# Windowed attention and a mixture of experts: the tiles that join two batches become plain 256-column tiles, in another order

## The chip, the cores and the metric

The kernel runs on one core of one Trainium2 chip. Its engines are TensorE (PE; its weight loads are listed apart as PEld), VectorE (DVE), ScalarE (ACT), GpSimd (POOL) and SyncE (SP, which issues most DMAs). The metric is the device time of one execution in microseconds (us), lower is better.

## The reference

In short: causal attention with a window of 128 keys and a bias by distance, and then a mixture of experts in which each token goes to one expert.

```python
batch, n_heads, seq, head_dim = (4, 8, 576, 64)
...
scores = scale * np.matmul(q, k.transpose(0, 1, 3, 2))
rel = pos[:, None] - pos[None, :]
bias = slopes[:, None, None] * (-np.abs(rel).astype(np.float32))[None, :, :]
mask = (rel >= 0) & (rel < window)
scores = np.where(mask, scores + bias[None], -1000000000.0)
attn = softmax(scores)
x = np.matmul(attn, v)
...
N, D, E, F = (2304, 512, 8, 1024)
expert_idx = np.argmax(x @ w_gate, axis=1)
h = np.maximum(np.einsum('ecd,edf->ecf', disp, w1), 0.0)
y = np.einsum('ecf,efd->ecd', h, w2)
out[i] = gate_w[i] * y[expert_idx[i], pos[i]]
```

## The kernel before

**Tiles.** 576 rows of a batch are four tiles of 128 rows and a rest of 64. The rests of two batches share one tile of 128 rows, the joined tile (`i == 4` in `TILES`), so there are 18 tiles: for each pair of batches nine, the fifth of them joined (numbers 4 and 13). A query row sees at most 128 keys back, so tile i needs the keys of chunks i-1 and i: 256 columns, and 128 in the four first tiles of a batch.

**Steps of a tile.** `turn_raw` turns raw k and q by products with the identity; `turn_hi` (ACT) and `turn_lo` (DVE) split the turned block into two f16 parts. `qk` makes scores of four heads into two PSUM banks, with three f16 products for each head (high-high, low-high, high-low); the two heads of a 128-row chunk lie in rows 0 to 63 and 64 to 127 of PE and come in pairs in the trace (x2). `softmax` (DVE) adds the table `tab` of bias and mask and finds the largest score, `expo` (ACT) makes `p`. For two heads at a time, `ptrans` turns `p` on PE into `pt`, `pevac` copies it into `pT`, and `pv` multiplies by v (65 columns: v and a column that sums). `xden`, `xrec`, `xnorm` divide, `xput` writes the rows to `xd` in DRAM, `xtrans`, `xevac`, `logits` make the gate's logits. An f32 product of `pv`, `logits` is two passes in the trace.

**The joined tile before.** `qM` and `pM` are 256 wide with zeros, so that queries of batch z stand in their 64 columns of block z and zeros elsewhere. `qk` runs each product for both batches on 192 keys (128 of chunk 3 and the last 64) into the same columns. `pv` then has four products for each head, two of them with 64 rows:

```python
ops = [(z, *x) for z in range(2 if i == 4 else 1) for x in key_chunks(ti)]
for y, (z, ci, vi, n) in enumerate(ops):
    PE.matmul(
        xv[:, h % 4, 0:D + 1], lhsT=s["pT"][:n, ci, a, 128 * z:128 * z + 128], rhs=vS[:n, (b0 + z) % 2, vi, h, 0:D + 1],
```

**Routing and experts.** When the rows of a batch of tiles have logits, `route_ops` ranks them (`o_rank` on PE), and POOL, PE and DVE make lists of tokens by expert. After the third of five batches (tiles 9 to 12 and half of 13) the first two experts begin: `gather` of their rows, `x_hi`, `x_lo`, two DMA transposes (`x_tr`), and `up` (PE, line 743). The weights of these two are split into f16 parts (`w_hi` on ACT, `w_lo` on DVE, line 677 and 681) during attention.

**Order.** Everything up to the first two experts is planned by `Plan`: each step has an engine, a time and a key; a list scheduler with a model of the clock, of transfers and of queues runs in the program's build and puts the steps of each engine in the order in which it would start them. Keys are shifted by the table `KEYS`. On the chip each engine takes its steps in that order, whatever time they need. The other six experts follow in written order.

**Lines on PE.** `turn_raw` 287, `qk` 331, `ptrans` 361, `pv` 387, `xtrans` 421, `logits` 443, `o_rank` 498, `o_list` 571, `up` 743; in the changed kernel 293, 339, 369, 393, 424, 446, 501, 574 and 746. `softmax` is line 346, `x_hi` 710, `x_tr` 719.

Of the kernel before, what the change touches and what calls it, by code (L numbers as in the profile page):

```python
# [43 lines left out]
C_N = C_T + 448  # L44
# [136 lines left out]
def attention_moe(ctx, tc, q, k, v, w_gate, w1, w2, capacity, const, out):  # L181
# [24 lines left out]
    tab = cp.tile([128, H, 448], BF16, name="tab")  # L206
# [16 lines left out]
    vS = kt.tile([128, 2, 5, H, DV], F32, name="vS")  # L223
# [18 lines left out]
    def setup_v():  # L242
        POOL.memset(vS[:, :, :, :, D:DV], 1.0 / XS)
# [930 lines left out]
```

## Time and profile before

| | us |
|---|---|
| median of 3 runs (lowest to highest) | 486.26 (482.13 to 494.63) |
| the profiled execution, its own time | 487.78 |
| its span (first to last instruction) | 486.0 |
| PE busy, DVE busy, ACT busy | 448.7, 245.0, 236.3 |
| attention, until the first expert's first product | 241.4 |

The profiled execution lies 1.5 us above the median of the runs, and 1.8 us of its time lie outside its span. [...] A busy PE in the profile includes pipelined instructions that overlap, so it shows where PE idles rather than how fast it works.

### The profile page before, as it was taken

To read this page: it belongs to the slowest core of one execution; us is meant where nothing else is said; L and a number is where in the kernel's file an instruction comes from. 1 tells how busy PE (TensorE), PEld (TensorE's weight loads), DVE (VectorE), ACT (ScalarE), POOL (GpSimd) and SP (SyncE) were. 2 spreads that over 40 slices of the span, in tenths; PEclk is the share of its full clock that TensorE was granted. 3 is DMA by queue.
4 is the path that set the end of the run, shared out by engine and by line. 5 is a ranking of instruction groups with operands and counts; after the bars stand their busy time and mean duration, and the time that the engine had idled before them with its cause. 6 is when DMAs were issued, how large, how long until landed. Compare 5 with 4: busy or idle time off the path is not lost. (4 is left out here: it accounts for less than half of the span.)

```text
span 486.0 us, 9350 instructions
## 1 busy us (share of the span) xinstructions
PE 448.7 (92%) x3536; PEld 346.6 (71%) x3536; DVE 245.0 (50%) x735; ACT 236.3 (49%) x533; POOL 80.1 (16%) x107
## 2 busy tenths in 40 slices
PE   1799999999999999998999999999989999797991
PEld 1589977989889788788885766656838576465660
DVE  3587611678786313678363204381655528383410
ACT  1488613678777323577213215371755527474410
POOL 2000000004160000161405022300303121101010
PEclk9899956599999755568599999999998999999997
DMA  9996723555844001043769613577597836936010
GB/s 186 201 194 164 186 69 84 156 174 132 236 90 132 24 1 23 22 134 128 191 140 312 119 45 106 206 226 252 170 225 274 262 136 190 317 135 142 1 45 17
DMA packets 104282, 71.04 MB, mean 146 GB/s; under 512 B 86558, under 2 KB 86942, under 8 KB 104224
## 3 DMA queue, kind: packets, MB, share of 16 engines
q1 hardware_dynamic: 100624, 59.28, 46.1%
q0 software_dynamic: 3600, 11.03, 7.3%
q8 instruction: 32, 0.52, 0.5%
q14 instruction: 26, 0.21, 0.1%
HBM read 54.55 MB, written 10.23 MB: 133 GB/s over the span
## 5 line engine op out<-in xcount | busy, mean ns | idle before, releaser
L743 PE MATMUL sc<-xTl,w1h 128*128 128x256 f16 (+1 forms) x320 | 82.3, 267 | 4.5 <-DMA xTl<-xgl 4.5
L743 PE MATMUL sc<-xTh,w1h 128*128 128x256 f16 (+1 forms) x320 | 82.3, 267 | 3.3 <-PEq L1118 1.8
L743 PE MATMUL sc<-xTh,w1l 128*128 128x256 f16 (+1 forms) x320 | 82.2, 267 | 0.0
L743 PEld LDWEIGHTS <-w1h 128*128 128x128 f16 x640 | 60.7, 100 | 13.4 <-issue 2.9
L387 PE MATMUL xb<-vS,pT 128*128 128x65 f32 x448 | 65.2, 299 | 2.5 <-issue 1.0
L387 PEld LDWEIGHTS xb<-vS,pT 128*128 128x128 f32 x448 | 62.0, 217 | 5.3 <-issue 2.0
L354 ACT ACTIVATE p<-sc,nm 128x256 f32<-128x256 f32 (+2 forms) x144 | 59.2, 452 | 4.3 <-DVE nm L346 2.4
L781 PEld LDWEIGHTS <-hh 128*128 128x128 f16 x336 | 32.6, 98 | 36.8
L346 DVE CUSTOM_DVE_ANT_0 sc<-sc,tab 128x256 f32<-128x256 f32 (+2 forms) x144 | 53.8, 398 | 9.5 <-PE sc L331 6.8
L681 DVE SCALAR_TENSOR_TENSOR w2l<-wr,w2h 128x512 f16<-128x512 f32 x64 | 43.2, 686 | 25.9 <-ACT w2h L677 25.9
L361 PE MATMUL pt<-cst,p 128*128 128x128 f32 (+1 forms) x256 | 47.0, 314 | 1.8 <-ACT p L354 1.1
L762 DVE SCALAR_TENSOR_TENSOR hl<-sc,hh 128x512 f16<-128x512 f32 x36 | 24.7, 690 | 47.3 <-ACT hh L758 46.6
L681 DVE SCALAR_TENSOR_TENSOR w1l<-wr,w1h 128x512 f16<-128x512 f32 x64 | 41.1, 691 | 11.9 <-ACT w1h L677 11.9
L758 ACT ACTIVATE hh<-sc 128x512 f16<-128x512 f32 x36 | 21.4, 596 | 50.1 <-PE sc L743 50.0
L788 POOL DMA_INDIRECT out_dram<-ys,sidx x17 | 17.0, 999 | 150.4 <-ACT ys L785 121.4
L677 ACT ACTIVATE w2h<-wr 128x512 f16<-128x512 f32 x64 | 38.8, 625 | 1.6 <-ACTq L1118 1.6
L361 PEld LDWEIGHTS pt<-cst,p 128*128 128x128 f32 (+1 forms) x256 | 34.1, 164 | 5.7 <-ACT p L354 2.2
L743 PEld LDWEIGHTS <-w1l 128*128 128x128 f16 x320 | 31.9, 100 | 8.5 <-DVE w2l L681 5.0
L677 ACT ACTIVATE w1h<-wr 128x512 f16<-128x512 f32 x64 | 35.7, 622 | 0.0
L502 POOL TENSOR_TENSOR srun<-srun,oh 128x8 bf16<-128x8 bf16 (+1 forms) x20 | 4.5, 224 | 186.3 <-PE bank L498 185.1
L387 PE MATMUL xb<-vS,pm 64*128 64x65 f32 (+1 forms) x128 | 33.7, 389 | 0.0
L387 PEld LDWEIGHTS xb<-vS,pm 64*128 64x128 f32 (+1 forms) x128 | 27.8, 269 | 6.1 <-issue 0.4
(123 smaller groups left out, 811.0 us busy)
## 6 DMA issues: line engine op xcount, KB each, us to landing
wr<-in_moe_w_dram SPq DMA_DIRECT2D x32, 1024.0 KB, 5.8
qf<-in_q_dram SPq DMA_DIRECT2D x16, 256.0 KB, 3.5
vS<-in_v_dram SPq DMA_DIRECT2D x16, 256.0 KB, 4.3
kf<-in_k_dram SPq DMA_DIRECT2D x16, 256.0 KB, 4.9
xd<-xs SPq DMA_DIRECT2D x16, 256.0 KB, 4.0
vS<-in_v_dram SPq DMA_DIRECT2D x4, 128.0 KB, 3.8
qf<-in_q_dram SPq DMA_DIRECT2D x4, 128.0 KB, 4.0
kf<-in_k_dram SPq DMA_DIRECT2D x4, 128.0 KB, 5.4
```

Of the source, the lines that this page charges most:

```text
L346: DVE.tensor_tensor_reduce(out=sc, in0=sc, in1=tab[:, 2 * hp + a, o + c0:o + c1], scale=-0.125, scalar=3.0e38, op0=ALU.add, op1=ALU.min, a ...
L354: ACT.activation(out=s["p"][:, a, c0:c1], in_=sc_of(ti, hp, a)[:, c0:c1], func=ACTF.Exp, scale=-1.0, bias=s["nm"][:, a:a + 1])
L361: PE.transpose(s["pt"][:n, ci, a], s["p"][:, a, 128 * ci:128 * ci + n], ident)
L387: PE.matmul(xv[:, h % 4, 0:D + 1], lhsT=s["pT"][:n, ci, a, 128 * z:128 * z + 128], rhs=vS[:n, (b0 + z) % 2, vi, h, 0:D + 1], start=(y == 0 ...
L502: POOL.tensor_tensor(out=srun[p0:p1], in0=srun[p0:p1], in1=w["oh"][p0:p1, g], op=ALU.add)
L677: ACT.activation(out=hi, in_=src, func=ACTF.Copy, scale=WS)
L681: eng.scalar_tensor_tensor(out=lo, in0=src, scalar=WS, in1=hi, op0=ALU.mult, op1=ALU.subtract)
L743: PE.matmul(hp, lhsT=l[:, o], rhs=r[:, :, c], start=(c == 0 and y == 0), stop=(c == 3 and y == 2))
L758: ACT.activation(out=hh, in_=hp, func=ACTF.Relu)
L762: DVE.scalar_tensor_tensor(out=hl, in0=hp, scalar=0.0, in1=hh, op0=ALU.max, op1=ALU.subtract)
L781: PE.matmul(hid[key, "y", i], lhsT=l[:, f, 128 * i:128 * i + 128], rhs=r[:, o], start=(f == 0 and y == 0), stop=(f == 7 and y == 2))
L788: POOL.indirect_dma_start(out=out, out_offset=bass.IndirectOffsetOnAxis(ap=scol, axis=0), in_=hid[key, "ys", i], in_offset=None, bounds_ch ...
```

## The change

The joined tile becomes a tile of 256 key columns like the others. Its columns 128 to 255 hold the last 64 keys of the first batch and beside them those of the second; the table masks the other batch's. `qk` makes the first 128 columns for both batches as before, and each batch's 64 columns apart. The last 64 rows of v of the two batches are stacked in one slot of `vS`, rows 0 to 63 and 64 to 127, so that `pv` has three products of 128 rows for each head: two of `pM` (chunk 3 of either batch) and one of `pT` (the stacked chunk). The planner's `KEYS` are other numbers, and so are some constants of its model of PE, which act on the order alone.

```diff
@@ constants()
-    full = p[:, None] - np.arange(256)[None, :] + 128
-    rest = p[:, None] % 64 - np.arange(192)[None, :] + 128
+    q, col = p[:, None], np.arange(256)[None, :]
+    full = q - col + 128
+    rest = np.where(col < 128, full, np.where(col // 64 == 2 + q // 64, q % 64 - col % 64, -1))
+    rest = np.where(col < 128, q % 64 - col + 128, rest)
-    c[:, C_T:C_T + 448] = np.where((rel >= 0) & (rel < WIN), rel, 1.0e12)
+    c[:, C_T:C_T + 512] = np.where((rel >= 0) & (rel < WIN), rel, 1.0e12)
...
-KEYS = {'E0': -31.3, 'E1': -10.0, 'R0': 504.7, 'R1': -102.9, 'R2': -140.3, 'R4': -82.4,
...
+KEYS = {'E0': -195.9, 'E1': -59.9, 'R0': 998.6, 'R1': 463.7, 'R2': -597.3, 'R3': 16.7, 'R4': 21.2,
...
-    tab = cp.tile([128, H, 448], BF16, name="tab")
+    tab = cp.tile([128, H, 512], BF16, name="tab")
...
-    vS = kt.tile([128, 2, 5, H, DV], F32, name="vS")
+    vS = kt.tile([128, 9, H, DV], F32, name="vS")
...
-    pM = kt.tile([128, 2, 2, 256], F32, name="pm")
+    pM = kt.tile([128, 2, 256], F32, name="pm")
+
+    def v_at(b, i):
+        return vS[:, b % 2 * 4 + i if i < 4 else 8]
-            n = 128 if i < 4 else 64
-            SP.dma_start(out=vS[:n, b % 2, i, :, 0:D], in_=src[b, :, 128 * i:128 * i + n, :].rearrange("h p d -> p h d"))
+            p = slice(0, 128) if i < 4 else slice(64 * (b % 2), 64 * (b % 2) + 64)
+            SP.dma_start(out=v_at(b, i)[p, :, 0:D], in_=src[b, :, 128 * i:min(128 * i + 128, S), :].rearrange("h p d -> p h d"))
...
 
     def key_chunks(ti):
         i = TILES[ti][1]
-        if i == 0:
-            return [(1, 0, 128)]
-        return [(0, i - 1, 128), (1, i, 128 if i < 4 else 64)]
+        return [(1, 0)] if i == 0 else [(0, i - 1), (1, i)]
 
     def span(ti):
-        i = TILES[ti][1]
-        return 128 * (i == 0), 192 if i == 4 else 256
+        return 128 * (TILES[ti][1] == 0), 256
 
     def parts(ti):
         b, i = TILES[ti]
...
         c0, c1 = span(ti)
         for a in range(2):
             c = 2 * g + a
-            ops = [(z, l, r) for z in range(2 if i == 4 else 1) for l, r in ((0, 0), (1, 0), (0, 1))]
-            for x, (z, l, r) in enumerate(ops):
-                for y in range(2):
-                    d = slice(64 * y, 64 * y + 64)
-                    PE.matmul(
-                        ring[2 * (u % 2) + y][:, 256 * a + c0:256 * a + c1],
-                        lhsT=qM[l][d, c, 128 * z:128 * z + 128] if i == 4 else qT[q_ring(ti)][l][d, c],
-                        rhs=kT[r][d, (b0 + z) % 2, c, 128 * (i - 1) + c0:128 * (i - 1) + c1], start=(x == 0), stop=(x == len(ops) - 1),
-                    )
+            base = 256 * a - 128 * (i - 1)
+            groups = [([0], 128 * (i - 1) + c0, 128 * (i - 1) + c1, 0)]
+            if i == 4:
+                groups = [([0, 1], 384, 512, 0), ([0], 512, 576, 0), ([1], 512, 576, 64)]
+            for zs, k0, k1, off in groups:
+                ops = [(z, l, r) for z in zs for l, r in ((0, 0), (1, 0), (0, 1))]
+                for x, (z, l, r) in enumerate(ops):
+                    for y in range(2):
+                        d = slice(64 * y, 64 * y + 64)
+                        PE.matmul(
+                            ring[2 * (u % 2) + y][:, base + off + k0:base + off + k1],
+                            lhsT=qM[l][d, c, 128 * z:128 * z + 128] if i == 4 else qT[q_ring(ti)][l][d, c],
+                            rhs=kT[r][d, (b0 + z) % 2, c, k0:k1], start=(x == 0), stop=(x == len(ops) - 1),
+                        )
 
     def sc_of(ti, hp, a):
         return ring[2 * ((2 * ti + hp // 2) % 2) + a].rearrange("p (a n) -> p a n", a=2)[:, hp % 2]
...
         s = st[ti, hp]
         s["pt"] = ptb[z].rearrange("k (c a q) -> k c a q", c=2, a=2)
         for a in range(2):
-            for ci, vi, n in key_chunks(ti):
-                PE.transpose(s["pt"][:n, ci, a], s["p"][:, a, 128 * ci:128 * ci + n], ident)
-
-    def pt_views(ti, t, wide=False):
-        i = TILES[ti][1]
+            for ci, _ in key_chunks(ti):
+                PE.transpose(s["pt"][:, ci, a], s["p"][:, a, 128 * ci:128 * ci + 128], ident)
+
+    def pevac(ti, hp):
+        s, i = st[ti, hp], TILES[ti][1]
+        s["pT"] = pp.tile([128, 2, 2, 128], F32, tag="pT", name="pT", bufs=3)
+        pieces = [(s["pT"], s["pt"])] if 0 < i < 4 else [(s["pT"][:, 1], s["pt"][:, 1])]
         if i == 4:
-            if wide:
-                return [t[:n, ci].rearrange("k a (z n) -> k a z n", z=4)[:, :, 0:4:3] for ci, _, n in key_chunks(ti)]
-            return [t[:n, ci].rearrange("k a (z n) -> k a z n", z=2) for ci, _, n in key_chunks(ti)]
-        return [t[:, 1]] if i == 0 else [t]
-
-    def pevac(ti, hp):
-        s = st[ti, hp]
-        s["pT"] = pM if TILES[ti][1] == 4 else pp.tile([128, 2, 2, 128], F32, tag="pT", name="pT", bufs=3)
-        for x, pt in zip(pt_views(ti, s["pT"], True), pt_views(ti, s["pt"])):
+            wide = pM.rearrange("k a (z n) -> k a z n", z=4)[:, :, 0:4:3]
+            pieces.append((wide, s["pt"][:, 0].rearrange("k a (z n) -> k a z n", z=2)))
+        for x, pt in pieces:
             ACT.copy(out=x, in_=pt) if EVAC[hp] == "ACT" else DVE.tensor_copy(out=x, in_=pt)
 
     xv = xb[:, 0:4 * DV].rearrange("p (h d) -> p h d", h=4)
...
         b0, i = TILES[ti]
         for a in range(2):
             h = 2 * hp + a
-            ops = [(z, *x) for z in range(2 if i == 4 else 1) for x in key_chunks(ti)]
-            for y, (z, ci, vi, n) in enumerate(ops):
-                PE.matmul(
-                    xv[:, h % 4, 0:D + 1], lhsT=s["pT"][:n, ci, a, 128 * z:128 * z + 128], rhs=vS[:n, (b0 + z) % 2, vi, h, 0:D + 1],
-                    start=(y == 0), stop=(y == len(ops) - 1),
-                )
+            ops = [(s["pT"][:, ci, a], v_at(b0, vi)) for ci, vi in key_chunks(ti)]
+            if i == 4:
+                ops[0:1] = [(pM[:, a, 128 * z:128 * z + 128], v_at(b0 + z, 3)) for z in range(2)]
+            for y, (l, r) in enumerate(ops):
+                PE.matmul(xv[:, h % 4, 0:D + 1], lhsT=l, rhs=r[:, h, 0:D + 1], start=(y == 0), stop=(y == len(ops) - 1))
 
     def xden(ti, g):
         s = st[ti]
...
-        pT = "pm" if i == 4 else ("pT", n % 3)
+        pT = [("pT", n % 3)] + ["pm"] * (i == 4)
```

What that does to the order. PE, products of the fifth tile (the joined one; `pm` is `pM`, `pt` the turned `p`, `xs` the divided rows, `xT` those turned). Before, from the first product that reads `pM`:

```order
L387 MATMUL xb<-vS,pm 128x65 x8
L361 MATMUL pt_92<-cst,p 128x128
L361 MATMUL pt_92<-cst,p 64x128
L361 MATMUL pt_92<-cst,p 128x128
L361 MATMUL pt_92<-cst,p 64x128
L421 MATMUL bank<-cst,xs 128x128 x2
L443 MATMUL bank<-wgf,xT 128x8 x4
L387 MATMUL xb<-vS,pm 128x65 x8
```

and now, in the same tile, its second pair of heads to its fourth:

```order
L393 MATMUL xb<-vS,pm 128x65 x2
L393 MATMUL xb<-vS,pT 128x65
L393 MATMUL xb<-vS,pm 128x65 x2
L393 MATMUL xb<-vS,pT 128x65
L369 MATMUL pt_92<-cst,p 128x128 x4
L293 MATMUL pt_93<-cst,kf 128x128 x4
L424 MATMUL bank<-cst,xs 128x128 x2
L393 MATMUL xb<-vS,pm 128x65 x2
L393 MATMUL xb<-vS,pT 128x65
L393 MATMUL xb<-vS,pm 128x65 x2
L393 MATMUL xb<-vS,pT 128x65
```

Eight products for two heads became six, the 64-row forms are gone, and now two pairs of heads follow each other at once.

PE, the end of attention, up to the first product of the first expert (`w1h`, `xTh` and `xTl` are its weights and rows). Before:

```order
L361 MATMUL pt_93<-cst,p 128x128 x4
L421 MATMUL bank<-cst,xs 128x128 x2
L387 MATMUL xb<-vS,pT 128x65 x8
L421 MATMUL bank<-cst,xs 128x128 x2
L443 MATMUL bank<-wgf,xT 128x8 x4
L421 MATMUL bank<-cst,xs 128x128 x2
L443 MATMUL bank<-wgf,xT 128x8 x4
L743 LDWEIGHTS w1h
L743 MATMUL sc_90<-xTh_2785,w1h 128x256
```

and now:

```order
L369 MATMUL pt_92<-cst,p 128x128 x4
L369 MATMUL pt_93<-cst,p 128x128 x4
L424 MATMUL bank<-cst,xs 128x128 x2
L393 MATMUL xb<-vS,pT 128x65 x8
L446 MATMUL bank<-wgf,xT 128x8 x4
L746 LDWEIGHTS w1h
L746 MATMUL sc_90<-xTh_2783,w1h 128x256
L746 LDWEIGHTS w1h
L746 MATMUL sc_90<-xTl_2784,w1h 128x256
```

The expert's first product stood behind the last logits; now nine such products stand ahead of the last division, the last eight products with v and the last logits.

SP, the first loads (`cst` 128x128 is the identity, `wr` the table). Before:

```order
L276 DMA qf<-in_q_dram 128x8x64
L272 DMA vS<-in_v_dram 64x8x64
L272 DMA vS<-in_v_dram 128x8x64
L276 DMA kf<-in_k_dram 128x8x64
L226 DMA cst<-in_const_dram 128x128
L249 DMA wr<-in_const_dram 128x448
```

and now:

```order
L278 DMA vS<-in_v_dram 64x8x64
L278 DMA vS<-in_v_dram 128x8x64
L282 DMA kf<-in_k_dram 128x8x64
L282 DMA qf<-in_q_dram 128x8x64
L282 DMA kf<-in_k_dram 128x8x64
L229 DMA cst<-in_const_dram 128x128
L252 DMA wr<-in_const_dram 128x512
```

The identity moved from the fifth place to the sixth, behind two loads of k and one of q.

## Rows read from the trace of the kernel before

**Rows 1.** The page, 40 equal slices of the span: busy tenths, granted clock
```profile
PE   1799999999999999998999999999989999797991
...
PEclk9899956599999755568599999999998999999997
```

**Rows 2.** Stretches: width, busy us (count) of five engines, granted clock, DMA
```profile
61.40:81.40 20.00, 19.54 (x88) 15.42 (x88) 2.67 (x11) 4.44 (x13) 0.00 (x0) 0.50 0.25 62
...
84.80:95.20 10.40, 10.25 (x64) 9.21 (x64) 7.13 (x25) 6.43 (x18) 0.00 (x0) 0.51 0.56 148
95.20:163.60 68.40, 67.55 (x720) 61.03 (x716) 52.32 (x220) 50.87 (x135) 16.95 (x30) 1.00 0.52 146
163.60:191.00 27.40, 27.37 (x120) 22.42 (x120) 3.95 (x16) 6.28 (x19) 0.00 (x0) 0.50 0.00 0
191.00:214.30 23.30, 22.41 (x143) 18.92 (x144) 14.99 (x61) 14.04 (x35) 9.27 (x15) 0.50 0.26 69
214.30:228.60 14.30, 12.66 (x114) 10.97 (x110) 12.28 (x46) 11.83 (x30) 2.41 (x2) 0.98 0.40 129
228.60:241.40 12.80, 11.82 (x60) 11.32 (x60) 4.82 (x19) 3.48 (x9) 5.42 (x8) 0.50 0.63 164
```

**Rows 3.** The same, of the products that read `pm` alone, PE alone
```profile
58.00:85.00 27.00, 16.16 (x64) 0.62 0.39 97
61.40:81.40 20.00, 10.52 (x36) 0.50 0.25 62
159.00:190.00 31.00, 17.58 (x64) 0.57 0.03 10
163.60:191.00 27.40, 14.70 (x48) 0.50 0.00 0
```

**Rows 4.** The same, of the products that read `pT` alone, PE alone
```profile
95.20:159.00 63.80, 26.54 (x208) 1.00 0.55 152
189.00:214.30 25.30, 7.95 (x32) 0.50 0.24 64
```

**Rows 5.** Groups by shape: products of `pm`, busy us and mean ns of one
```profile
L387 PE MATMUL xb<-vS,pm 64*128 64x65 f32 x64 | 19.2, 394 | 0.0
...
L387 PE MATMUL xb<-vS,pm 128*128 128x65 f32 x64 | 18.5, 384 | 0.0
```

**Rows 6.** Timeline of PE, 150 to 159 us: start, length, count, score products
```profile
150.19 0.26 PE L331 MATMUL sc<-kTh,qmh 64*128 64x192 f16 x2
...
151.29 1.11 PE L387 MATMUL xb<-vS,pT 128*128 128x65 f32 x8
...
158.13 0.23 PE L331 MATMUL sc<-kTh,qh 64*128 64x128 f16 x2
...
158.57 0.44 PE L421 MATMUL bank<-cst,xs 128*128 128x128 f32 x2
```

**Rows 7.** Groups by shape: softmax on DVE, 256 and 192 columns
```profile
L346 DVE CUSTOM_DVE_ANT_0 sc<-sc,tab 128x256 f32<-128x256 f32 x96 | 39.6, 433 | 7.0 <-PE sc L331 4.6 <-ACT p L354 2.1
...
L346 DVE CUSTOM_DVE_ANT_0 sc<-sc,tab 128x192 f32<-128x192 f32 x16 | 5.6, 364 | 1.1 <-PE sc L331 0.9 <-ACT p L354 0.2
```

**Rows 8.** Timelines of PE, ACT, SP, from the third ranking to the first expert
```profile
198.93 0.21 PE L498 MATMUL bank<-oh,ub 128*128 128x8 bf16 x1
...
218.23 0.59 PE L571 MATMUL bank<-ohc,ohl 128*128 128x144 f16 x5
...
224.72 0.72 ACT L710 ACTIVATE xgh<-xg 128x512 f16<-128x512 f32 x1
...
228.78 0.73 ACT L710 ACTIVATE xgh<-xg 128x512 f16<-128x512 f32 x1
...
231.02 1.24 SPq L719 DMA_TRANSPOSE xTl<-xgl  x1
...
241.42 0.38 PE L743 MATMUL sc<-xTh,w1h 128*128 128x256 f16 x1
```

**Rows 9.** Timeline of PE, its first instruction
```profile
7.97 1.09 PE L287 MATMUL pt<-cst,kf 128*128 128x128 f32 x4 [7.97 <-DMA cst<-in_const_dram]
```

More of the change, by code (lines that the diff above doesn't have):

```diff
@@ L43 @@
 C_T = C_L1 + NTL
-C_N = C_T + 448
+C_N = C_T + 512
 TILES = [(b + x, i) for b in (0, 2) for x, i in [(0, 0), (0, 1), (0, 2), (0, 3), (0, 4), (1, 0), (1, 1), (1, 2), (1, 3)]]
@@ L86 @@
     WINDOW = 4096 / 1200
+    UP, STAY = 0.84, 0.35
     SAME = {"PE": 0.0, "DVE": 0.12, "ACT": 0.2, "POOL": 0.1, "SP": 0.0}
@@ L120, in window @@
     def window(self):
-        self.warm = self.busy > (0.46 if self.warm else 0.79) * self.WINDOW
+        self.warm = self.busy > (self.STAY if self.warm else self.UP) * self.WINDOW
         self.busy = 0.0
@@ L242, in setup_v @@
     def setup_v():
-        POOL.memset(vS[:, :, :, :, D:DV], 1.0 / XS)
+        POOL.memset(vS[:, :, :, D:DV], 1.0 / XS)
     stage = []
@@ L248, in table_load @@
         stage.append(wf.tile([128, 2048], F32, tag="wr", name="wr"))
-        SP.dma_start(out=stage[0][:, 0:448], in_=const[:, C_T:C_N])
+        SP.dma_start(out=stage[0][:, 0:512], in_=const[:, C_T:C_N])
     def setup_tab():
@@ L253, in setup_tab @@
             DVE.tensor_scalar(
-                out=tab[:, h], in0=stage[0][:, 0:448], scalar1=-8.0 * 2.0 ** -(h + 1), scalar2=None, op0=ALU.mult
+                out=tab[:, h], in0=stage[0][:, 0:512], scalar1=-8.0 * 2.0 ** -(h + 1), scalar2=None, op0=ALU.mult
             )
@@ L857, in plan_turn @@
         d = dests(x, b, i)
-        P.op("PE", 0.436, (key, n), turn_raw, x, b, i, z, r=[("r" + x, at[x, b, i]), "cst"], w=[("pt", z)])
+        P.op("PE", 0.436, (key, n), turn_raw, x, b, i, z, r=[("r" + x, at[x, b, i]), "cst"], w=[("pt", z)], rows=0.75)
         P.op("ACT", 0.482, (key + 0.4, n), turn_hi, x, b, i, z, r=[("pt", z)], w=[y + ("h",) for y in d])
@@ L882, in plan_qk @@
         X = 2 * (u % 2)
-        P.op("PE", 0.66 if 0 < i < 4 else 0.36 if i == 0 else 1.0, (2 * u, "qk"), qk, u, r=need(ti), w=[("sc", X), ("sc", X + 1)], rows=0.75)
+        P.op("PE", 0.66 if 0 < i < 4 else 0.36 if i == 0 else 1.0, (2 * u, "qk"), qk, u, r=need(ti), w=[("sc", X), ("sc", X + 1)], rows=1.2)
     def plan_step(ti, hp):
@@ L895, in plan_step @@
             P.op("ACT", 0.155 + (c1 - c0) / 1200, (n + 0.6 + 0.2 * a, "expo"), expo, ti, hp, a, r=[("sc", X + a), ("nm", PB, a)], w=[("p", PB, a)])
-        P.op("PE", 0.218 * len(ch), (n + 1.1, "ptrans"), ptrans, ti, hp, PT, r=[("p", PB, 0), ("p", PB, 1), "cst"], w=[("pt", PT)])
+        P.op("PE", 0.218 * len(ch), (n + 1.1, "ptrans"), ptrans, ti, hp, PT, r=[("p", PB, 0), ("p", PB, 1), "cst"], w=[("pt", PT)], rows=0.75)
         el, k = (256, 2) if i == 4 else (256 * len(ch), 1)
-        pT = "pm" if i == 4 else ("pT", n % 3)
+        pT = [("pT", n % 3)] + ["pm"] * (i == 4)
         act = EVAC[hp] == "ACT"
-        P.op("ACT" if act else "DVE", k * (0.055 + el / 1200 if act else 0.068 + el / 960), (n + 1.5, "pevac"), pevac, ti, hp, r=[("pt", PT)], w=[pT])
-        vs = [("v", b % 2, vi) for b, _, _ in parts(ti) for _, vi, _ in ch]
-        P.op("PE", 0.224 * len(ch) * (2 if i == 4 else 1), (n + 2.6, "pv"), pv, ti, hp, r=[pT, "vone"] + vs, w=["x"])
+        P.op("ACT" if act else "DVE", k * (0.055 + el / 1200 if act else 0.068 + el / 960), (n + 1.5, "pevac"), pevac, ti, hp, r=[("pt", PT)], w=pT)
+        vs = [("v", b % 2, vi) for b, _, _ in parts(ti) for _, vi in ch]
+        P.op("PE", 0.224 * len(ch) * (1.5 if i == 4 else 1), (n + 2.6, "pv"), pv, ti, hp, r=pT + ["vone"] + vs, w=["x"], rows=0.38)
         t2 = ti % 2
@@ L908, in plan_step @@
             P.op("DVE", 0.34, (n + 3.6, "xnorm"), xnorm, ti, g, r=["x", ("r", t2, g)], w=[("xs", t2, y) for y in range(g, 2)])
-            P.op("PE", 0.218, (n + 4.2, "xtrans"), xtrans, ti, g, r=[("xs", t2, g)], w=["xt"], bank=True)
+            P.op("PE", 0.218, (n + 4.2, "xtrans"), xtrans, ti, g, r=[("xs", t2, g)], w=["xt"], bank=True, rows=0.75)
             P.op("ACT", 0.265, (n + 4.6, "xevac"), xevac, ti, g, r=["xt"], w=[("xT", t2, y) for y in range(g, 2)], bank=True)
@@ L912, in plan_step @@
             P.op("SP", 0.55 * len(parts(ti)), (n + 4.0, "xput"), xput, ti, r=[("xs", t2, 0), ("xs", t2, 1)], w=[("xd", ti)], xfer=0.73, post=1.6)
-            P.op("PE", 0.45, (n + 5.0, "logits"), logits, ti, r=[("xT", t2, 0), ("xT", t2, 1), "cst2"], w=[("lg", region[x[0]]) for x in bof[ti]], bank=True, rows=0.13)
+            P.op("PE", 0.45, (n + 5.0, "logits"), logits, ti, r=[("xT", t2, 0), ("xT", t2, 1), "cst2"], w=[("lg", region[x[0]]) for x in bof[ti]], bank=True, rows=0.03)
     def plan_early():
```

2 lines of the change are left out of this document (1 added, 1 removed).

## The prediction

> **What bounds the kernel now.** I read the page's slices first. PE is busy nearly throughout, so the question is how fast it works; the row of the granted clock has two dips, slices 5 to 8 and 13 to 18, and a short one near slice 20 [rows 1]. Cutting the span where the clock changes gives the stages [rows 2]. [...]
>
> What did PE do before the clock fell? The two dips begin in the joined tiles: 58 to 85 us and 159 to 190 us hold all products that read `pM`, 64 passes each [rows 3]. The fall at 61.4 comes inside the first run of them, that at 84.8 right after the fourth, that at 163.6 soon after the fifth. In 95.2 to 163.6, with six plain tiles' worth of work, there is none. The last fall, at 228.6, follows a stretch in which PE idled 1.6 us of 14.3 [rows 2]: the end of attention, where DVE (12.28 of 14.30 us) and a chain of short steps set the pace.
>
> **What the pM products cost.** Their 128 passes take 16.16 + 17.58 = 33.7 us [rows 3]: 14.70 / 48 = 0.306 us each at 0.50, and (16.16 - 10.52) / 28 = 0.20 each outside the low stretch. A pass of `pT`, 128 rows and the same 65 columns, takes 26.54 / 208 = 0.128 us at 1.00 and 7.95 / 32 = 0.248 us at 0.50 [rows 4]. So passes that alternate between 64 and 128 rows cost 1.2 to 1.6 times a plain one. It isn't that only the 64-row ones are dear: both shapes show alike, 394 and 384 ns [rows 5], so what I blame is the alternation.
>
> **The change part by part.**
> (A) `pv` of the joined tiles: 128 passes of mixed rows become 96 of 128 rows, the shape of `pT`. At full clock 96 x 0.128 = 12.3 us in place of 33.7: 21.5 us less. At low clock 96 x 0.248 = 23.8: 9.9 less. I take the first, for the reason in (B).
> (B) The rest of PE's work in the low stretches of the joined tiles. Without their pM passes (10.52 and 14.70 us, rows 3) the stretches of 20.0, 10.4 and 27.4 us hold 9.5 + 10.4 + 12.7 = 32.6 us. A pT pass at 1.00 takes half of one at 0.50, so at full clock this is 16.3 us less. That the clock stays up is the main choice here. For it: every fall near a joined tile came in or just after a run of pM passes, and runs of pT passes of the plain tiles were followed by none in 68 us. Against: the joined tile still has more `pv` than a plain one (12 passes for two heads in place of 8), and two pairs of heads now follow each other without other work between.
> (C) The tail, 191 to 241.4 us, 50.4 us. At full clock PE's part shrinks, but not the chain from the third ranking to the first expert: 198.93 to 241.42, 42.5 us [rows 8]. The first expert's second transpose goes out at 231.02; in the chain I see waits that a faster PE and an order that puts these steps sooner can take away (the list product waits for its place on PE until 218.23; the second `x_hi` stands until 228.78, 3.3 us after the first one ends at 225.44). The other floor is DVE: 14.99 + 12.28 + 4.82 = 32.1 us of work, at the 86% of the stretch 214.3 to 228.6 [rows 2] 37.4 us, and some 4 us for the chain's end. That gives 41.4 in place of 50.4, 9 us less. Ends: 0 (the chain as long as it was) and 18 (DVE's bare 32). The nine expert products that now stand ahead of the last `pv` wait for those transposes, and behind them in PE's queue stand the last division's transposes, the last eight `pv`, the last logits and the fifth ranking; if the chain is late, that is where PE stands, and the gain of this part is gone.
> (D) `qk` of the joined tiles: 48 pairs of 192 columns become 48 of 128 and 48 of 64. A pair of 192 takes (151.29 - 150.19) / 12 = 0.092 us with the handover, one of 128 (158.57 - 158.13) / 6 = 0.073 [rows 6]. A pair of 64 columns isn't in the trace: between half of 0.073 and all of it, since it loads as many weights; not less, as its columns are half. So 4.4 us become 3.5 + 1.8 to 3.5: 0.9 to 2.6 us more. No row is nearer to either end, I take 1.7.
> [...]
> (E) The start: PE's first instruction waits for the identity until 7.97 us [rows 9]. It is now the sixth load, and one more block of k and of q is turned ahead of the first scores, 1.09 us a block at this clock, of which the work comes off later. I take 1 us more, ends 0 and 2.2.
> (F) `softmax` of the joined tile on 256 columns: 16 x (433 - 364) ns = 1.1 us on DVE [rows 7], and as much or less on ACT. Nothing on the path while DVE has the room of rows 2; 1 to 2 us if it hasn't. The table is 64 columns wider; pM's second copy is now one into `pT` of the same columns: nothing.
>
> **The sum.** 487.8 (the profiled execution) - 21.5 - 16.3 - 9 + 1.7 + 1 = 443.7. That execution lies 1.5 us above the median of the runs, so I say **443 us**. Its own range: 18 in (C) and the lower ends of (D) and (E) give 433; nothing in (C) and the upper ends 455.
>
> **The rivals.**
> 1. *The clock falls all the same.* A run of `pv` passes as such may bring it down, of whatever rows. With both falls as before, (A) gives 9.9 and (B) and (C) nothing: 487.8 - 9.9 + 2.7 = 480.6; with (C) 471.6; middle 476. With one fall of the two: 443.7 + 5.7 (48 passes at 0.248, not 0.128) + 10 (half of 9.5 + 10.4, the first tile) = 459, or for the second tile 5.7 + 6.4 and half of the tail's gain, 460. For it: low clock, once there, lasted 10 to 51 us [rows 2], so one slip is dear.
> 2. *The alternation isn't what costs.* If a pass has its price whatever its rows are, as the two rows 394 and 384 alone would say [rows 5], 96 x 0.264 = 25.3 us: 8.4 less, the clock falls as before, and the time is 482. Against it stand rows 4 with the same shape at half to four fifths of the price.
> [...]
> 3. *Slower: low clock where there was none.* Everything is in another order, and nothing shows that the plain tiles keep their clock in it. One more fall as long as the longest seen (50.7 us, half of it lost) on top of rival 1 without (C): 480.6 + 25.3 = 506. It decides from 34 us of additional low clock, if rival 1 holds, and from over 100 us if it doesn't. For it: the low stretch after the second joined tile went on through 23.3 us of plain tiles, so these don't raise the clock quickly. Against: no fall in the 68 us of rows 2.
>
> **How the numbers follow.** Forecast 0.55; one fall remains 0.18; both 0.11; rival 2 0.06; slower 0.06; 0.04 for what I don't see. A measurement of this kernel can tell about 2%, 9.7 us, from no change: below 476.5 is faster. Forecast, one fall and half of both: faster 0.79. The other half, rival 2 and a bit: same 0.14. Slower 0.07. The range goes from the forecast's 433, a little lower for a tail without any wait, to 478, which takes in one fall and most of both.
>
> **What would show it.** Passes of `pM` and `pT` in the joined tiles at 0.13 us each in a run, 1.00 in the clock row where slices 5 to 8 and 13 to 16 were low, and the first expert's first product near 198 us in place of 241; the experts after it keep their 245 us. A step is wrong if the joined tiles' passes take 0.2 us at full clock (A), if the clock falls inside their `pv` runs or at the logits behind them (B), or if PE stands before the first expert's products for more than 10 us (C). The forecast as a whole fails if plain tiles lose the clock.

## The result, and the profile of the changed kernel

| | us, median (lowest to highest) | against the kernel before |
|---|---|---|
| before | 490.29 (482.13 to 494.63), 4 runs | |
| changed | 452.22 (448.35 to 457.28), 4 runs | 0.931, 95% interval 0.917 to 0.946 |

The change makes the kernel faster by 5 to 8%. The ratio, like every ratio with an interval further on, compares the faster executions of each kernel (three of the changed one and two of the one before here); the quotient of the two medians is 0.922. The profiled execution took 457.28 us (span 455.4) and is the longest of the four, so places in the trace are up to 5 us later than in a middling run.

The page of the changed kernel, the row of the granted clock, to be held against [rows 1]:

```profile
PEclk9999999999999967569999999999989999899997
```

Counted from 1, the dips of [rows 1] are slices 6 to 8, 14 to 18 and 20, where the forecast has 5 to 8 and 13 to 18. Those of the joined tiles are gone; what is left of low clock lies in slices 15 to 18, the end of attention. Stretches of it, to be held against [rows 2] (width, busy us and count of PE, PEld, DVE, ACT and POOL, granted clock, DMA share, GB/s); the first two hold both joined tiles' `pv`:

```profile
55.00:95.00 40.00, 39.33 (x410) 35.49 (x410) 30.12 (x118) 29.81 (x82) 3.26 (x9) 1.00 0.79 209
145.00:154.00 9.00, 9.00 (x94) 8.29 (x93) 4.28 (x19) 4.95 (x17) 0.00 (x0) 1.00 0.02 4
154.00:163.00 9.00, 8.17 (x100) 6.82 (x99) 7.52 (x33) 7.37 (x20) 1.61 (x4) 1.00 0.13 29
163.00:178.00 15.00, 12.53 (x66) 10.73 (x66) 10.89 (x39) 9.88 (x22) 10.48 (x12) 0.54 0.62 159
178.00:184.00 6.00, 3.96 (x36) 2.92 (x34) 5.89 (x17) 5.04 (x12) 2.67 (x2) 1.00 0.33 88
184.00:202.00 18.00, 17.68 (x97) 16.68 (x97) 8.04 (x41) 8.52 (x21) 4.66 (x8) 0.53 0.45 89
```

At full clock (1.00) PE idles where DVE and ACT set the pace (178 to 184: DVE busy 5.89 of 6.00 us); behind this stretch the clock is at 0.53 and PE is the bound (17.68 of 18.00). The timeline of PE: the first product of all, two early score products, the split score products and what stands behind them, the first of a step's 12 `pv` passes and what stands behind the last, what stands behind the joined tiles' last `pv`, the first expert product, and a stretch of attention behind the first nine expert products:

```profile
9.02 1.09 PE L293 MATMUL pt<-cst,kf 128*128 128x128 f32 x4 [9.02 <-DMA cst<-in_const_dram]
...
24.26 0.42 PE L339 MATMUL sc<-kTh,qh 64*128 64x256 f16 x2
24.47 0.42 PE L339 MATMUL sc<-kTh,ql 64*128 64x256 f16 x2
...
48.21 0.23 PE L339 MATMUL sc<-kTh,qmh 64*128 64x128 f16 x2
...
48.56 0.19 PE L339 MATMUL sc<-kTh,qmh 64*128 64x64 f16 x2
...
48.73 0.22 PE L339 MATMUL sc<-kTh,qmh 64*128 64x128 f16 x2
...
49.34 0.44 PE L424 MATMUL bank<-cst,xs 128*128 128x128 f32 x2
...
147.25 0.66 PE L393 MATMUL xb<-vS,pm 128*128 128x65 f32 x4
...
148.63 1.04 PE L369 MATMUL pt<-cst,p 128*128 128x128 f32 x8
...
153.78 0.39 PE L369 MATMUL pt<-cst,p 128*128 128x128 f32 x2
...
202.94 0.27 PE L746 MATMUL sc<-xTh,w1h 128*128 128x256 f16 x1
...
203.92 0.38 PE L424 MATMUL bank<-cst,xs 128*128 128x128 f32 x2
...
205.87 0.27 PE L746 MATMUL sc<-xTh,w1h 128*128 128x256 f16 x1
```

A step's 12 passes take 148.63 - 147.25 = 1.38 us, 0.115 us each from start to start. In the kernel before, the row behind the joined tiles' last `pv` is this:

```profile
189.09 1.12 PE L361 MATMUL pt<-cst,p 128*128 128x128 f32 x4
```

So that `pv` is done at 153.78 in place of 189.09, 35.3 us earlier; the first expert product comes at 202.94 in place of 241.42 [rows 8], 38.5 us earlier; the end only 30.6 us earlier (spans 486.0 and 455.4). The two first expert products do not stand at the same place, though: in the new order 3.0 us of attention's work on PE come behind that product (203.92 to 205.87, 207.96 to 208.18 and 209.16 to 209.97: two divisions' transposes, the last `pv`, the last logits), and in the old order none. What PE waited for from 130 us on (in total, times, longest):

```profile
PE sc L746 <- DMA xTl<-xgl: 8.5, 3, 3.4
PE pt L369 <- ACT p L362: 4.2, 4, 1.8
PE sc L784 <- DVE hl L765: 2.5, 1, 2.5
```

So there are three things to explain: what the tile gave, what the new order gave, and where 8 us went behind the first expert product.

### The profile page after: what moved, and what is told of

Same layout as the page of the kernel before. It is cut to its first block, busy times and chain, and to the rows that moved or that the text cites. A ratio compares the mean times of both kernels' runs of the same rounds, so it can differ in the third digit from the quotient of the medians.

```text
span 455.4 us, 9461 instructions
## 1 busy us (share of the span) xinstructions
PE 411.2 (90%) x3600; PEld 317.2 (70%) x3600; DVE 246.5 (54%) x735; ACT 236.8 (52%) x533; POOL 81.6 (18%) x107
## 5 line engine op out<-in xcount | busy, mean ns | idle before, releaser
L393 PE MATMUL xb<-vS,pT 128*128 128x65 f32 x480 | 67.8, 290 | 0.6 <-issue 0.6
L393 PEld LDWEIGHTS xb<-vS,pT 128*128 128x128 f32 x480 | 64.9, 211 | 1.1 <-issue 0.9
L362 ACT ACTIVATE p<-sc,nm 128x256 f32<-128x256 f32 (+1 forms) x144 | 60.8, 459 | 5.2 <-DVE nm L354 4.8
L354 DVE CUSTOM_DVE_ANT_0 sc<-sc,tab 128x256 f32<-128x256 f32 (+1 forms) x144 | 54.6, 409 | 10.3 <-PE sc L339 5.5
L369 PE MATMUL pt<-cst,p 128*128 128x128 f32 x256 | 45.5, 306 | 4.4 <-ACT p L362 4.2
L680 ACT ACTIVATE w2h<-wr 128x512 f16<-128x512 f32 x64 | 38.5, 624 | 3.7 <-DMA wr<-in_moe_w_dram 2.1
L746 PEld LDWEIGHTS <-w1l 128*128 128x128 f16 x320 | 31.7, 99 | 12.3 <-issue 7.1
L369 PEld LDWEIGHTS pt<-cst,p 128*128 128x128 f32 x256 | 33.0, 163 | 10.4 <-ACT p L362 6.7
L379 ACT COPY pT<-pt 128x512 f32<-128x512 f32 (+1 forms) x54 | 27.8, 517 | 13.7 <-PE pt L369 10.2
L784 PEld LDWEIGHTS <-hl 128*128 128x128 f16 x168 | 16.4, 98 | 21.5 <-DVE hl L765 1.9
```

The lines of the kernel that those rows point to most:

```text
L354: DVE.tensor_tensor_reduce(out=sc, in0=sc, in1=tab[:, 2 * hp + a, o + c0:o + c1], scale=-0.125, scalar=3.0e38, op0=ALU.add, op1=ALU.min, a ...
L362: ACT.activation(out=s["p"][:, a, c0:c1], in_=sc_of(ti, hp, a)[:, c0:c1], func=ACTF.Exp, scale=-1.0, bias=s["nm"][:, a:a + 1])
L369: PE.transpose(s["pt"][:, ci, a], s["p"][:, a, 128 * ci:128 * ci + 128], ident)
L379: ACT.copy(out=x, in_=pt) if EVAC[hp] == "ACT" else DVE.tensor_copy(out=x, in_=pt)
L393: PE.matmul(xv[:, h % 4, 0:D + 1], lhsT=l, rhs=r[:, h, 0:D + 1], start=(y == 0), stop=(y == len(ops) - 1))
L680: ACT.activation(out=hi, in_=src, func=ACTF.Copy, scale=WS)
```

## The experiments

Both kernels plan the same 1,315 steps, so the tile and the order can be exchanged. "Order" below means this list of steps, replayed word for word. Times are compared within one chip, each group of kernels beside runs of the kernel before there; across chips only by the ratio to it.

### The tile and the order, each alone

```diff
+SEQ = [
...
-        for i in order:
+        for i in SEQ:
             ops[i][3](*ops[i][4])
```

`SEQ` is the list of the kernel before, put into the changed kernel (new tile, old order), and the other way round (old tile, new order).

New tile, old order:

> The changed joined tile with every instruction planned in the order of the kernel before, step for step. Theory T (the tile's mixed passes cost time and bring the clock down): the pm and pT passes of the joined tiles take 0.11 to 0.13 us each, the clock stays at 1.00 up to the last of them, the last pm product ends some 35 us earlier than before (near 154 us), and the time is 440 to 455 us; if the tail of the old order is the better one, at the lower end. Rival O (the new order is what keeps the clock up): the clock falls near 60 and 160 us as before and the time is 472 to 482 us.

Old tile, new order:

> The joined tile of the kernel before, with every instruction planned in the order of the changed kernel. Theory T: the clock falls again in or behind the runs of mixed passes, the passes take 0.2 us at full clock and 0.3 at low, and the time is 480 to 495 us. Rival O: the clock stays up through both joined tiles, the 128 passes cost 0.2 us each in place of 96 at 0.107, so 15 us on top of the changed kernel: 463 to 468 us.

Measured: 445.13 us (444.4 to 449.01) and 477.64 us (476.19 to 481.36), the kernel before on this chip 483.18 (473.27 to 490.71): 0.921 and 0.989 of it by the medians. PE alone in the joined tiles (width, busy us and count, granted clock, DMA share, GB/s), first the new tile in the old order:

```profile
55.00:95.00 40.00, 38.96 (x391) 0.96 0.71 190
145.00:154.00 9.00, 9.00 (x86) 1.00 0.01 2
```

and the old tile in the new order:

```profile
55.00:95.00 40.00, 40.00 (x280) 0.74 0.52 134
145.00:177.00 32.00, 32.00 (x251) 0.81 0.09 26
```

The tile alone gives the whole gain. The order alone gives nothing that these times show: its 476.19 to 481.36 us lie inside the range of the kernel before (and under the 480 to 495 of theory T). In the second pair PE idles nowhere, and the clock falls all the same: it needs no wait of PE's for that. The new tile in the old order has a short fall in the first tile (40 x 0.04 x 2 = 3 us of low clock), behind this wait of PE's, and is else at 1.00 there:

```profile
59.61 1.06 PE L496 MATMUL bank<-wgf,xT 128*128 128x8 f32 x8 [0.46 <-ACT xT L480]
```

A second profile of the same kernel has the same wait of 0.46 us at 59.50 us and no fall, so the wait doesn't decide it, and what does isn't shown:

```profile
55.00:95.00 40.00, 38.95 (x412) 1.00 0.74 196
```

### Which part of the tile: the rows of a pass

Three kernels change nothing but the rows of the joined tiles' four passes a head in the kernel before. Rows of zeros below the 64-row products:

```diff
+        POOL.memset(vS[64:128, :, 4, :, 0:D], 0.0)
...
-            for y, (z, ci, vi, n) in enumerate(ops):
+            for y, (z, ci, vi, _) in enumerate(ops):
+                n = 128
```

> The kernel before, with the 64-row products of the joined tiles made 128 rows by rows of zeros: still four passes a head, 128 in all, all of 128 rows. Theory T (alternation of 64 and 128 rows costs): 128 passes at 0.11 to 0.13 us, 14 to 16 us in place of 33.7, the clock stays at 1.00 in the joined tiles, and the time is 448 to 462 us. Rival (a pass of pm has its price whatever its rows): no change, 0.2 to 0.31 us a pass, 482 to 492 us. Rival (rows cost, but a run of pv passes as such brings the clock down): passes at 0.25 us at low clock, falls as before, 474 to 482 us.

Order 128, 128, 64, 64:

```diff
-            ops = [(z, *x) for z in range(2 if i == 4 else 1) for x in key_chunks(ti)]
+            ops = [(z, *x) for x in key_chunks(ti) for z in range(2 if i == 4 else 1)]
```

> The kernel before, with the four passes of a head in the order 128, 128, 64, 64 rows in place of 128, 64, 128, 64: the same passes, half the changes of row count. If each change of row count costs (0.07 to 0.1 us by the price of a mixed pass less that of a plain one at full clock): half of it goes, a pass takes 0.16 to 0.17 us at full clock, the clock may fall once or not at all, and the time is 455 to 478 us. If the 64-row passes themselves cost: no change, 482 to 492 us.

All at 64 rows; this kernel leaves the upper 64 keys of chunk 3 out of the sums:

```diff
             for y, (z, ci, vi, n) in enumerate(ops):
+                n = 64 if i == 4 else n
```

> The kernel before with all four passes a head of the joined tiles at 64 rows, so that no pass of another height lies between them (the upper 64 keys of the block before are left out of the sums). If the change between row counts costs: 128 passes at 0.11 to 0.13 us, 14 to 17 us, the clock stays up in the joined tiles, 450 to 462 us. If a 64-row pass is dear by itself: 0.2 us a pass or more at full clock, 25 us or more in all, and the clock falls as before, 475 to 492 us.

Measured: padded 449.78 us (447.55 to 451.02), grouped 477.22 (476.4 to 480.88), beside 483.18; all at 64 rows, one execution on another chip, 467.57, between its two expectations, the kernel before there 487.08. One run of 16 passes of each at full clock (a group is printed with its first pass's shape), and what stands behind it. First the kernel before, from a second profile of it (below):

```profile
78.16 2.88 PE L387 MATMUL xb<-vS,pm 128*128 128x65 f32 x16
80.97 0.66 PE L361 MATMUL pt<-cst,p 128*128 128x128 f32 x4
```

grouped:

```profile
56.88 2.42 PE L387 MATMUL xb<-vS,pm 128*128 128x65 f32 x16
59.23 0.66 PE L361 MATMUL pt<-cst,p 128*128 128x128 f32 x4
```

padded:

```profile
58.49 2.00 PE L389 MATMUL xb<-vS,pm 128*128 128x65 f32 x16
60.33 0.60 PE L362 MATMUL pt<-cst,p 128*128 128x128 f32 x4
```

all at 64 rows:

```profile
58.72 1.95 PE L388 MATMUL xb<-vS,pm 64*128 64x65 f32 x16
60.59 0.66 PE L361 MATMUL pt<-cst,p 128*128 128x128 f32 x4
```

Start to start 2.81, 2.35, 1.84 and 1.87 us: 0.176, 0.147, 0.115 and 0.117 us a pass. A product's two passes have the same rows and come one behind the other in the trace, so the 16 passes are 8 products. Against the padded run, 8 changes of row count (the one to the transposes behind counted in) cost 0.97 us and 4 cost 0.51, 0.121 and 0.128 each; the 0.07 to 0.1 of the expectation took a change at every pass. A 64-row pass among its like costs what a full one does (0.117 and 0.115 us); the change between the two costs, 0.12 to 0.13 us here.

The four rows agree with one price for each change; what PE does in that time isn't shown.

The clock doesn't follow that price alone. PE in the joined tiles of the padded kernel:

```profile
55.00:95.00 40.00, 38.81 (x389) 0.96 0.69 181
145.00:159.00 14.00, 14.00 (x144) 1.00 0.06 21
```

of the grouped one:

```profile
55.00:95.00 40.00, 39.50 (x259) 0.66 0.50 129
145.00:180.00 35.00, 35.00 (x266) 0.70 0.08 24
```

and with all at 64 rows:

```profile
55.00:95.00 40.00, 39.08 (x336) 0.83 0.60 151
145.00:164.00 19.00, 19.00 (x198) 1.00 0.04 16
```

Half the changes are half the surcharge, but the clock is about as low as in the first profile of the kernel before, and the time is within 1.3% of that kernel's. Passes of 64 rows at the plain price let it fall too, in their one profile (0.83 in the first tile; in the second it falls behind the last of them). With rows of zeros it stays up but for a short fall. So full rows do two things: no changes, and no long fall. In all nine profiles here with full rows the granted clock from 55 to 95 us is 0.96 or more, in the five with 64-row passes 0.62 to 0.87. Why passes of 64 rows let it fall isn't shown.

### The kernel before, once more

No edit.

> The kernel before, profiled once more, for two readings. PE's waits for the third experts' transposes (xTl): 4.5 us in its first profile, 4.8 to 5.9 on one chip whatever the order, 7.4 to 8.7 on the two others whatever the order and in the changed kernel's first profile. If they belong to the chip and not to the new order, this run shows 7 us or more, unless it falls on a chip like the first. If they belong to the order: 4.5 to 6 us on any chip. And the low stretches of the joined tiles, 20 + 10 us and over 20 us, come back at the same places (near 60, 85 and 160 us); if they are chance, they move.

Measured: 477.09 us. PE in its joined tiles:

```profile
55.00:95.00 40.00, 38.99 (x304) 0.87 0.56 139
145.00:177.00 32.00, 32.00 (x236) 0.77 0.08 24
```

The falls come back in the same tiles, but how long they last differs: 40 x 0.13 x 2 = 10.4 us of low clock in the first tile, where the first profile had some 30 [rows 2]. The kernel before ran from 473 to 496 us over all runs here, with a mean granted clock of 0.929 in the shortest and 0.882 in the longest; falls of unequal length would do that. The waits for `xTl` are 5.8 us, which decides nothing between chip and order.

### What the new order costs

The changed kernel and the new tile in the old order, side by side on one chip, five rounds; no edits beyond those above.

> The changed kernel itself, on one chip with the next two, to price its order against the old one. Theory N (the new order gives back what it should have brought: PE waits 4.2 us for the exponentials in the tail, 2.5 us for the second expert's hidden layer, and more for the transposes): 1.3 to 2.2% slower than the changed tile in the old order. Rival S (the difference of 7 us between the two medians is one between chips): within 0.7% of it.

> The changed tile in the order of the kernel before, on the same chip. Theory N: 6 to 10 us under the changed kernel, 0.92 to 0.925 of the kernel before. Rival S: within 3 us of the changed kernel.

Measured: 452.92 us (447.23 to 458.63), 0.941 of the kernel before (0.933 to 0.949), and 447.76 us (445.18 to 453.78), 0.932 (0.926 to 0.938). The new order is 5 us slower by the medians, a little less than theory N expected. The two intervals overlap, so that it costs 1% is likely and not shown; that it gains anything is not seen. Both profiles of the changed kernel are of the longest execution of their group, so the prices read from them are high ones. With the old order the first expert product comes earlier, and one wait is smaller and one absent. The timeline of its first profile, and of its waits from 150 us on that for the exponentials:

```profile
198.78 0.37 PE L796 MATMUL sc<-xTh,w1h 128*128 128x256 f16 x1
```

```profile
PE pt L419 <- ACT p L412: 0.9, 1, 0.9
```

198.78 against 202.94, 0.9 us of waiting for the exponentials against 4.2, and none for the second expert's hidden layer (2.5 us). In the two profiles of these five rounds it is 196.85 against 201.35, 0.9 us against 4.9, and none against 2.8.

### Trying to mend the tail and the second expert

Four kernels move steps, nothing else. The first, from the new tile in the old order, moves some thirty; of PE's row:

```diff
+L443 MATMUL xb<-vS,pT 128x65 x8
+L419 MATMUL pt_93<-cst,p 128x128 x4
 L624 LDWEIGHTS ohl
 L624 MATMUL bank<-ohc,ohl 128x144
...
-L419 MATMUL pt_93<-cst,p 128x128 x4
-L443 MATMUL xb<-vS,pT 128x65 x8
```

> The changed tile in the old order, with some thirty steps moved: logits of the fourth tile behind the joined tile's second pv, and in the tail the weight splits of the second expert (four of ACT and of DVE) behind the last tiles' softmax, that softmax, its exponentials and their transposes up front, and four pv ahead of the list product that waits for POOL. Theory W (PE's waits of 1.7, 0.9 and 0.45 us there are what the clock falls after, near 185 us): PE idles 3 us less between 170 and 190 us, the low clock of 17 us goes or halves, the one near 62 us (3.4 us) goes, and the time is 4 to 11 us under the old order with the changed tile. Rival (the tail is a chain of short steps whose order doesn't matter): within 2 us, the clock falls near 185 us again.

Measured: 453.89 us, 0.944 (0.936 to 0.952), beside 447.76 without the moves. The short fall near 62 us came too (0.96 from 55 to 95 us), though the wait for `xT` ahead of it was gone. In the tail the moves had put an evacuation, two exponentials and `x_hi` ahead of a division's `xden` on ACT (its timeline), PE waited 3.0 us for what follows from it on DVE, and the clock fell there again (PE alone):

```profile
183.08 0.58 ACT L429 COPY pT<-pt 128x512 f32<-128x512 f32 x1 [2.81 <-PE pt L419]
183.71 0.86 ACT L412 ACTIVATE p<-sc,nm 128x256 f32<-128x256 f32 x2
184.46 0.71 ACT L763 ACTIVATE xgh<-xg 128x512 f16<-128x512 f32 x1
...
185.32 0.18 ACT L448 ACTIVATE dn<-xb 128x4 f32<-128x4 f32 x1
```

```profile
PE xb L443 <- DVE eq L530: 3.0, 1, 3.0
```

```profile
185.00:206.00 21.00, 17.59 (x90) 0.51 0.45 130
```

The second moves only ACT's and DVE's last weight splits, one pair of exponentials, one division and one tile's logits, ACT's row:

```diff
 xevac(15, 0)
+expo(17, 2, 0)
+expo(17, 2, 1)
-w_hi(1, 8)
-w_hi(1, 9)
 xevac(15, 1)
-w_hi(1, 10)
-w_hi(1, 11)
 x_hi((0, 0), 0)
...
 xden(17, 1)
+w_hi(1, 8)
+w_hi(1, 9)
 xevac(17, 0)
 xevac(17, 1)
+w_hi(1, 10)
+w_hi(1, 11)
```

> The changed tile in the old order with fewer moves than the reordered tail had: the list product and the gathers stay where they were, only the last weight splits of the second expert (four on ACT, four on DVE) go behind the last tile's steps, the exponentials of its third pair of heads and one division go ahead of x_hi, and the logits of the fourth tile behind the joined tile's second pv. Theory W (the waits of 0.9 and 0.45 us before 185 us bring the clock down): PE idles under 0.5 us between 178 and 190 us, the low clock of 17 us is shorter or gone, 438 to 444 us. Rival (the clock falls there whatever these waits are): 17 us of low clock again, 443 to 449 us.

Measured, on another chip: 451.73 us, 0.939 (0.933 to 0.945). That is no faster than without the moves (0.932). The wait for the exponentials went, one of 1.5 us for DVE took its place, and the clock fell at the same point:

```profile
PE xb L443 <- DVE d L525: 1.5, 1, 1.5
```

```profile
184.50:202.00 17.50, 16.52 (x86) 0.51 0.58 152
```

The third holds the same eight splits back in the changed kernel's own order:

```diff
 expo(17, 3, 1)
 xden(16, 1)
+w_hi(1, 8)
+w_hi(1, 9)
...
 xevac(16, 1)
+w_hi(1, 10)
+w_hi(1, 11)
```

> The changed kernel in its own order, but for the same eight weight splits held back behind the last tile's softmax and exponentials. Theory N (the splits stand ahead of the exponentials that PE waits for, 0.66, 1.3 and 0.4 us from 180 to 185 us, and the clock falls after them): these waits go, the first expert starts 2 to 8 us earlier than in the changed kernel, and the time is 444 to 450 us. Rival (other steps on ACT, the exponentials themselves among them, are what PE waits for): no change within 2 us, 450 to 455 us.

Measured: 455.34 us, 0.947 (0.939 to 0.955), no faster than the changed kernel (0.941), and nearly all of the 4.2 us is still there:

```profile
PE pt L419 <- ACT p L412: 4.1, 3, 1.9
```

So it isn't these splits that the exponentials stand behind; theory N is wrong in that. None of the three left PE without waits there, so whether the clock would stay up without them isn't shown.

The fourth moves `x_hi` of the third expert's blocks (and `x_lo` on DVE) behind the second expert's `relu`; ACT's row:

```diff
-x_hi((2, 0), 0)
 relu_hi((1, 0), 5)
-x_hi((2, 0), 1)
-x_hi((2, 0), 2)
+x_hi((2, 0), 0)
 relu_hi((1, 0), 7)
+x_hi((2, 0), 1)
+x_hi((2, 0), 2)
```

> The changed kernel in its own order, but for the gathered blocks of the third expert, whose x_hi and x_lo go behind the relu of the second expert's hidden layer in place of ahead of it. Theory N: PE's wait of 2.5 to 2.8 us for that hidden layer goes, and the time is 2 to 3 us under the changed kernel, 449 to 451 us. Rival (the third expert's blocks come later and are waited for in their turn): the wait moves to the third expert's first products, and the time is within 1 us of the changed kernel.

Measured: 455.02 us (447.88 to 456.36), 0.937 (0.923 to 0.952). PE's waits from 130 us on:

```profile
PE sc L796 <- DMA xTl<-xgl: 8.5, 3, 3.7
PE pt L419 <- ACT p L412: 4.1, 4, 1.8
```

The wait of 2.5 us is gone and no other has grown by it: the cause is shown, `x_hi` of blocks still on their way stood ahead of the `relu`. Its worth in time is below what these runs resolve.

## Why the prediction was right, and where it wasn't

**What bounds the kernel, and what to blame.** Right. PE bounds the joined tiles (busy 19.54 of 20.00 and 27.37 of 27.40 us at 0.50 [rows 2]), and the alternation of row counts is what costs there: padding alone, with all four passes kept, gives 33 of the 38 us that the new tile gives on that chip (449.78 and 445.13 against 483.18).

**(A) 96 passes for 128.** Right in kind, a little small in size: 96 x 0.115 = 11.0 us, where the forecast had 12.3. The busy time of a pass, 0.128 from [rows 4], was too much; 0.115 from start to start is the better price.

**(B) The clock stays up.** Right, 1.00 in both joined tiles, but for 3 us in one of the two profiles of the old order. The reason given (runs of mixed passes bring it down) holds with the old tile in the new order, but it is too narrow: passes that are all of 64 rows let the clock fall too (0.83 from 55 to 95 us). The 16.3 us belong to one execution, though; in another profile of the kernel before the falls were shorter (10.4 us in place of some 30 in the first tile).

**(C) The tail, 9 us.** This is the step that failed. From the end of the joined tiles' `pv` to the first expert product it took 241.42 - 189.09 = 52.3 us before and 202.94 - 153.78 = 49.2 after, 3 us less, and the 3.0 us of attention that now stand behind that product take this back: nothing is left of the 9. With the old order it is 198.78 - 153.34 = 45.4 (its last `pv` of the joined tiles is done at 153.34), 7 less, with all of attention in it. The forecast let PE run at full clock there and took DVE's work as the floor. But it had itself read a fall, at 228.6, behind a stretch in which PE idles [rows 2], and put none into the new tail. In the changed kernel 31 of these 49 us are at low clock (two stretches above), and so it is in all four profiles of the new tile in the new order. With full rows and the old order, in five profiles (two of them with the moved steps), it is 14 to 20 us; the least of it is in the new tile's first one:

```profile
153.34:198.78 45.44, 39.29 (x319) 0.85 0.46 122
```

What brings the clock down in the tail isn't shown; in the changed kernel both low stretches follow one in which PE idles (busy 8.17 of 9.00 and 3.96 of 6.00 us). The sign that the forecast named for (C), PE standing more than 10 us ahead of the expert's products, did not come.

**Behind the first expert product** the forecast left 245 us as they were. It took 252.5 (455.4 - 202.94) after 244.6 (486.0 - 241.42). Of the 8 us, 3.0 are the steps of attention that the new order has put there, 2.5 the `relu` behind `x_hi`, both prices of the new order; some 1.8 come off, as the first 17 expert products no longer run at low clock (0.21 us each from start to start before, 0.11 now). Another 4 are waits for the third experts' transposes, 8.5 us in place of 4.5. These went by chip more than by order: 4.8 to 5.9 us in the four kernels of one chip, 7.4 to 8.6 in four of the second, 8.3 to 8.7 in three of the third, with both orders among each. What sets them stays open.

**(D) The split score products.** +1.7 us forecast. A run of twelve pairs of 128 and twelve of 64 columns takes 49.34 - 48.21 = 1.13 us with the handover, the twelve pairs of 192 took 151.29 - 150.19 = 1.10 [rows 6]: over four runs 0.1 us more, below the lower end. Six pairs of 128 take 48.56 - 48.21 = 0.35 us and six of 64 take 48.73 - 48.56 = 0.17, 0.058 and 0.028 each; the forecast's 0.073 for a pair of 128 had the handover to another kind of product in it. Its bounds for a pair of 64, half of that and all of it, were the author's estimate, and 0.028 lies below both.

**(E) and (F).** PE's first instruction is 1.05 us later, 9.02 for 7.97 [rows 9], as forecast. The first score product is 3.0 us later, 18.44 for 15.46, above the upper end of 2.2, and the products keep half their pace for longer. A pair of 256 columns takes 24.47 - 24.26 = 0.21 us there and 0.11 from 27 us on; before, the slow pace lasted until 16.5 us and came back from 20 to 23.3 (granted clock 0.50, a low stretch that [rows 2] leaves out). The column of the granted clock reads 1.00 at such a start (7.9 to 16.5 us before, 9 to 27 now), so it is the distance of the starts that shows it. PE's work at half pace is 13.2 us in place of 8.5; half of the difference, an estimate of 2.3 us, is what this costs. The joined tiles' softmax is not seen on the path: from 55 to 95 us PE waited 0.7 us, for ACT alone, and from 145 to 154 not at all.

**The sum.** 443.7 for this execution, 457.3 measured: +6 in (C), +8 behind it, -3 in (A) and (D), and some 3 us more ahead of the last `pv`, most of which the slow start under (E) would account for. The median, 452.2, lies within the forecast's own 433 to 455.

**The rivals.** The clock that falls all the same did not come in the joined tiles; the tail's low clock is a case that this rival did not speak of. That the alternation isn't what costs is refuted by the padded rows (0.115 us a pass in place of 0.176). The slower case, low clock in plain tiles, did not come: between the slow start and the tail the granted clock is 1.00 (27 to 163.6 us).

**The order** was not a term of its own in the forecast. It should have been: the tile alone is the gain, and the version with the old order has the lowest median, 0.932 of the kernel before against 0.941. An estimate of what the new order costs: its tail has 31 us of low clock in place of 14 to 20, and half of the difference is 5 to 8 us.

## What to carry to other kernels

Keep all passes of an accumulation at one row count: here padding with rows of zeros cost nothing that these rows show (0.115 us a pass, 0.117 with 64 rows), and every change cost 0.12 to 0.13 us. When a stretch is freed from low clock, don't take the full clock for granted in the next: here the tail kept 31 us of low clock, behind stretches in which PE idles (8.17 of 9.00 and 3.96 of 6.00 us busy). Price a new layout and a new order apart, by replaying the old order.

## What the runs showed of the chip beyond that

Between f32 products of 65 columns, two passes each, a change of row count cost 0.12 us at full clock where every product changes it, and 0.13 where every second one does. With all passes at 64 rows, at the plain price and PE busy 39.08 of 40 us, the granted clock has a mean of 0.83; with rows of zeros below the 64, PE busy 38.81, it is 0.96 (one profile each). The waits for three transposes came to 4.5 to 8.7 us with the same instructions.
